# A two-layer transformer kernel whose softmax exponentials are shared by two engines: the first MLP weight streamed, two polynomial chains in flight, eight heads begun early, and a longer planned latency for a broadcast

## The chip, the cores and the metric

The kernel runs on one core of one Trainium2 chip. The metric is the device time of one launch in microseconds (us), median of several runs. The core has a matrix engine (TensorE, "PE" in the profile, "PEld" for its weight loads), a vector engine (VectorE, "DVE"), an activation engine (ScalarE, "ACT"), a general one (GpSimd, "POOL") and DMA queues; here almost all DMAs are issued from the sync queue ("SPq"). "PEclk" or "the granted clock" is the share of full clock that TensorE was given. The program gives each engine one order of instructions, and that order is fixed when it is built. In the traces a VectorE instruction that waits holds up those behind it (2.91 us at 465 us, shown in the prediction).

## The reference

Two identical layers; S = 2048 rows, D = 512, 32 heads of 16, MLP width 1792, bf16:

```python
def _A_ref(x, wqkv, wo):                     # attention
    qkv = (x @ wqkv).reshape(B, S, 3, H, Dh).transpose(2, 0, 3, 1, 4)
    q, k, v = qkv[0], qkv[1], qkv[2]
    scores = einsum("bhqd,bhkd->bhqk", q, k) * (Dh ** -0.5)
    o = einsum("bhqk,bhkd->bhqd", softmax(scores), v)
    return o.transpose(0, 2, 1, 3).reshape(B, S, D) @ wo
def _B_ref(x, w1, w2):                       # MLP
    return einsum("bsf,fd->bsd", maximum(einsum("bsd,df->bsf", x, w1), 0), w2)
for _ in range(2):
    x = x + _A_ref(layernorm(x), wqkv, wo)
    x = x + _B_ref(layernorm(x), w1, w2)
```

32 heads x 2048 x 2048 scores x 2 layers are 268 million exponentials: 4096 blocks of 128 x 512.

## The kernel before

The rows are cut into four chunks of 512. A *segment* is four heads of one chunk of queries over all 16 row blocks of keys: 64 score blocks. Three blocks make one ScalarE instruction. The kernel's source is a list scheduler: while it emits instructions it keeps a planned clock for PE and one for DVE (`now_pe`, `now_dve`), notes when each product will be ready, and picks the next instruction for each engine. The plan lives at build time alone; on the chip only the order is left of it. `mark` puts a product on the plan's clock, `at` asks for it:

```python
def mark(key, engine="dve", lag=0.0):
    made[key] = (engine, (now_pe if engine == "pe" else now_dve)[0] + lag)

def run_dve(until, musts):                   # which instruction VectorE gets next
    while True:
        can = [(0, m[1], m) for m in musts[:1]]
        if now_dve[0] < until:
            can += [(1, e[1], None) for e in list(evac)[:1]]
            for t in dve_q:
                ready = at(t["deps"], "dve")
                if ready is not None:
                    can.append((2, ready, t))
        ...                                  # [cut] those ready within 40 ns, by kind
```

The end of a segment: the sums of the softmax lie in four rows of the copied output `u`. They are gathered to 128 lanes (`c`), inverted, written back and broadcast to all lanes (`r`), then multiplied. The broadcast is planned to be there 5.5 us after the reciprocal:

```python
def copy():
    ...                                      # [cut] u <- ps_o
    nc.sync.dma_start(out=c[:], in_=sums)    # sums = u[lane:P:32, :]
    mark(("c", n), lag=2600.0)
def recip():
    nc.vector.reciprocal(out=c[:], in_=c[:])
    nc.sync.dma_start(out=sums, in_=c[:])
    nc.sync.dma_start(out=r[:], in_=bass.AP(tensor=sums.tensor, offset=sums.offset,
                      ap=[list(sums.ap[0]), [0, 32], [1, QS]]))
    mark(("r", n), lag=5500.0)
...
task(250, recip, [("r", n)], [("c", n)])
task(700, lambda: mul(0, QS), ots + [("m", n)], [("r", n)] + war)
```

VectorE takes some blocks off ScalarE, in pairs. `first_step` reads the scores; then a *chain* of five instructions on 128 x 1024 makes the exponential as a polynomial. Only one pair can be under way, and only in the first part of a segment:

```python
elif (not pairs and r <= LAST_PAIR
      and now_dve[0] + sum(...) < now_pe[0] + BACKLOG):   # [cut]
    half = 0
...
steps = ((690, bits dm), (1260, step dy), (1260, step dy), (1260, step de), (690, bits di))
task(cost, fn, [k], [...], place=n)          # chains go to the front of the queue
```

Layer 2 cannot start until the last chunk of layer 1 has passed its MLP and its keys and values are made. To fill that time, the first six "heads" (`NACC = 6` tiles of four heads each) of layer 2 run on the 12 row blocks of chunks 0 to 2 (*early* row blocks), their partial outputs are put into the chain's own buffers, and the four *late* row blocks follow in short segments of 16 blocks.

The softmax here doesn't subtract the row's maximum and nothing guards it: scores larger than these inputs give would overflow.

## Time and profile before

| | before |
|---|---|
| time, median of 4 runs in the rounds of the comparison | 1899.84 us (1899.27 to 1901.33) |
| profiled span, granted clock | 1896.0 us, 0.976 |
| exponentials on ScalarE: busy, idle before them | 1740.3 us, 20.9 us |
| VectorE busy, blocks taken from ScalarE | 1149.9 us (61%), 232 of 4096 |
| span = start + exponential loop + tail | 67.7 + 1761.2 + 67.0 |

The prediction below shows the lines. In a group line, "1740.3, 1589 | 20.9 <-PE" is busy us, mean ns of one, and us for which the engine stood idle just before, with what ended most of that idling.

### The profile page before, as it was taken

To read this page: it belongs to the slowest core of one execution; us is meant where nothing else is said; L and a number is where in the kernel's file an instruction comes from. 1 tells how busy PE (TensorE), PEld (TensorE's weight loads), DVE (VectorE), ACT (ScalarE), POOL (GpSimd) and SP (SyncE) were. 2 spreads that over 40 slices of the span, in tenths; PEclk is the share of its full clock that TensorE was granted. 3 is DMA by queue.
4 is the path that set the end of the run, shared out by engine and by line. 5 is a ranking of instruction groups with operands and counts; after the bars stand their busy time and mean duration, and the time that the engine had idled before them with its cause. 6 is when DMAs were issued, how large, how long until landed. Compare 5 with 4: busy or idle time off the path is not lost.

```text
span 1896.0 us, 29515 instructions
## 1 busy us (share of the span) xinstructions
PE 1654.1 (87%) x12867; PEld 520.5 (27%) x12867; DVE 1149.9 (61%) x1741; ACT 1764.1 (93%) x1407; POOL 2.4 (0%) x35
## 2 busy tenths in 40 slices
PE   4788888998989998999999878989988998899976
PEld 2222222222222222222222222222222222222222
DVE  4465657766676776776532335676657665666552
ACT  2799999999999999999999989999999999999950
POOL 0000000000000000000000000000000000000000
PEclk9899999999999999999999989999999999999998
DMA  4000000000000000000000010000000000000000
GB/s 166 1 12 7 13 13 13 8 12 12 11 9 13 13 10 10 13 13 13 10 3 1 4 30 11 13 12 10 19 15 13 7 15 21 13 8 12 21 10 11
DMA packets 34133, 29.39 MB, mean 16 GB/s; under 512 B 17492, under 2 KB 25428, under 8 KB 34004
## 3 DMA queue, kind: packets, MB, share of 16 engines
q1 hardware_dynamic: 32420, 25.94, 5.8%
q8 instruction: 100, 1.64, 0.4%
q10 hardware_dynamic: 1584, 1.57, 0.2%
q14 instruction: 29, 0.24, 0.0%
HBM read 7.86 MB, written 2.10 MB: 5 GB/s over the span
## 4 chain that ended last, share of the span: by engine, by line
ACT 83%; PE 8%; DVE 4%; DMA 3%; issue 1%; SPq 0%; DVEq 0%
ACT e L870 83%; PE ps_s L849 2%; DMA r<-u 2%; PE ps_f L347 2%; PE ps_s L347 2%; PE ps_o L668 1%; PE ps_s L789 1%; DMA u<-c 1%; DVE stats L364 1%; ACT xnT L783 0%; PE ps_s L401 0%; DVE ot L628 0%; DMA x<-in_A_x_dram 0%; DVE q L481 0%; DVE ktp L446 0%
## 5 line engine op out<-in xcount | busy, mean ns | idle before, releaser
L870 ACT ACTIVATE e<-ps_s 128x1536 bf16<-128x1536 f32 (+1 forms) x1366 | 1740.3, 1589 | 20.9 <-PE ps_s L849 19.8
L849 PE MATMUL ps_s<-q,ktp 32*128 32x512 bf16 x6503 | 720.3, 385 | 171.5 <-ACT e L870 135.7
L668 PE MATMUL ps_o<-e,vaug 128*32 128x512 bf16 x3864 | 547.2, 394 | 9.2 <-DVE u L617 7.2
L849 PEld LDWEIGHTS <-ktp 32*128 32x128 bf16 x6503 | 233.1, 92 | 633.7 <-issue 539.2
L707 DVE TENSOR_SCALAR di<-ps_s 128x512 int32<-128x512 f32 x232 | 159.7, 688 | 319.8 <-PE ps_s L849 319.1
L668 PEld LDWEIGHTS <-vaug 128*32 128x32 bf16 x4560 | 162.4, 93 | 466.3 <-issue 440.6
L738 DVE SCALAR_TENSOR_TENSOR dy<-dm 128x1024 f32<-128x1024 f32 x116 | 142.1, 1225 | 3.7
L738 DVE SCALAR_TENSOR_TENSOR de<-dy,di 128x1024 bf16<-128x1024 f32 x116 | 141.8, 1223 | 2.9
L738 DVE SCALAR_TENSOR_TENSOR dy<-dy,dm 128x1024 f32<-128x1024 f32 x116 | 141.7, 1221 | 2.6
L347 PE MATMUL ps_f<-w,ht 128*128 128x512 bf16 x406 | 120.0, 384 | 0.6 <-DVE x L528 0.5
L347 PE MATMUL ps_f<-xn2T,w 128*128 128x512 bf16 x400 | 117.7, 386 | 0.7
L514 DVE TENSOR_SCALAR ht<-ps_f 128x512 bf16<-128x512 f32 x99 | 68.2, 689 | 82.5 <-PE ps_f L347 81.0
L732 DVE TENSOR_SCALAR dm<-di 128x1024 int32<-128x1024 int32 x116 | 80.3, 692 | 3.5
L732 DVE TENSOR_SCALAR di<-di 128x1024 int32<-128x1024 int32 x116 | 80.3, 692 | 3.2
L668 PE MATMUL ps_o<-de,vaug 128*32 128x512 bf16 x464 | 79.3, 382 | 0.0
L347 PE MATMUL ps_f<-xnT,wqkv 128*128 128x512 bf16 x248 | 74.1, 390 | 1.2
L628 DVE SCALAR_TENSOR_TENSOR ot<-u,mask,r 128x512 bf16<-128x512 f32 (+1 forms) x67 | 48.4, 722 | 36.1 <-DMA r<-u 33.4
L347 PE MATMUL ps_f<-wo,ot 128*128 128x512 bf16 x224 | 67.7, 388 | 1.1
L617 DVE COPY u<-ps_o 128x512 f32<-128x512 f32 x58 | 40.0, 690 | 41.3 <-PE ps_o L668 41.2
L481 DVE TENSOR_SCALAR q<-ps_f,qmask 128x512 bf16<-128x512 f32 x68 | 48.6, 742 | 14.6 <-PE ps_f L347 14.5
L668 PE MATMUL ps_o<-di,vaug 128*32 128x512 bf16 x232 | 54.7, 391 | 0.0
L499 DVE TENSOR_TENSOR x<-x,ps_f 128x512 bf16<-128x512 bf16 x28 | 19.1, 684 | 57.6 <-PE ps_f L347 57.5
(67 smaller groups left out, 483.6 us busy)
## 6 DMA issues: line engine op xcount, KB each, us to landing
r<-u SPq DMA_DIRECT2D x63, 256.0 KB
w<-in_B_w_dram SPq DMA_DIRECT2D x2, 1792.0 KB
x<-in_A_x_dram SPq DMA_DIRECT2D x16, 128.0 KB
out_dram<-x SPq DMA_DIRECT2D x16, 128.0 KB
wqkv<-in_A_wqkv_dram ACTq DMA_DIRECT2D x3, 512.0 KB
c<-u SPq DMA_DIRECT2D x63, 8.0 KB
u<-c SPq DMA_DIRECT2D x63, 8.0 KB
wo<-in_A_wo_dram SPq DMA_DIRECT2D x1, 512.0 KB
```

The source lines that it names most:

```text
L347: nc.tensor.matmul(b, lhsT, rhs, start=(i == 0), stop=(i == n - 1))
L481: nc.vector.tensor_scalar(out=qbuf[n % 2][e][:], in0=b, scalar1=qmask[e][:, 0:1], scalar2=None, op0=ALU.mult,)
L499: nc.vector.tensor_add(out=x_t[tt][:], in0=x_t[tt][:], in1=b)
L514: nc.vector.tensor_scalar(out=ht[ft][:], in0=b, scalar1=0.0, scalar2=None, op0=ALU.max)
L617: nc.vector.tensor_copy(out=u[:], in_=ps_o[:])
L628: nc.vector.scalar_tensor_tensor(out=ot[t][:, a : a + w], in0=u[:, a : a + w], scalar=mask[e][:, 0:1], in1=r[:, a : a + w], op0=ALU.mult, ...
L668: nc.tensor.matmul(ps_o[32 * g : 32 * g + 32, :], vaug[sg["l"]][kb][:, 4 * sg["T"] + g, 2 * e : 2 * e + 32], rhs, start=g not in sg["begun ...
L707: first = nc.vector.tensor_scalar(out=di[:, half, :].bitcast(I32), in0=src, scalar1=EXP_BIAS, scalar2=0.0, op0=ALU.add, op1=ALU.max,)
L732: nc.vector.tensor_scalar(out=out[:].bitcast(I32), in0=di[:].bitcast(I32), scalar1=keep, scalar2=put, op0=ALU.bitwise_and, op1=ALU.bitwise_or,
L738: nc.vector.scalar_tensor_tensor(out=out[:], in0=x[:], scalar=c, in1=y[:], op0=ALU.add, op1=ALU.mult)
L849: nc.tensor.matmul(b[:, w, :], kt[32 * g : 32 * g + 32, kc : kc + P], qbuf[sg["n"] % 2][sg["e"]][32 * g : 32 * g + 32, :], start=True, sto ...
L870: ex = nc.scalar.activation(out=eb[:, :m, :], in_=b[:, :m, :], func=ACTF.Exp, scale=1.0 / (LOG2E * UNIT),)
```

## The change

Four things: W1 (1.8 MB) is no longer resident but streamed in blocks of 128 columns through four buffers; two chains may be outstanding, with a new rule for starting a pair; eight heads instead of six begin on the early row blocks; and the planned latency of the broadcast goes from 5.5 to 8.5 us. The intent is to move more blocks from ScalarE, which bounds the kernel, to VectorE. The diff, cut:

```diff
-    NACC = 6
+    NACC = 8
+    NW1 = 4
-    LAST_PAIR = 12
-    BACKLOG = 3000.0
+    SPREAD = 1.3
+    LATE = 0.0
+    BACKLOG = 6000.0
-    w1 = sb([P, NDC, DFF], BF16, "w1")
+    w1buf = [sb([P, NDC, P], BF16, f"w1_{n}") for n in range(NW1)]
-    di = sb([P, 2, QS], FP32, "di")
+    dis = [sb([P, 2, QS], FP32, f"di{n}") for n in range(2)]
-    acc = [x[:, k, :] for x in (dm, dy, di) for k in range(2)]
+    acc = [x[:, k, :] for x in [dm, dy] + dis for k in range(2)]
+    def load_w1(n):
+        if n < 2 * NQS * NF:
+            ft = n % NF
+            nc.sync.dma_start(out=w1buf[n % NW1][:],
+                in_=B_w1[:, ft * P : (ft + 1) * P].rearrange("(c p) f -> p c f", p=P))
+            mark(("w1", n), "pe", 4000.0)
     # [cut] h_group uses w1buf[n % NW1], and reloads it after its last matmul
-            mark(("r", n), lag=5500.0)
+            mark(("r", n), lag=8500.0)
     # [cut] di is handed on with the pair
-            task(cost, fn, [k], [key + (n - 1,)] if n else [], place=n)
+            task(..., place=sum("chain" in t for t in dve_q))
+            maker[k]["chain"] = True
-            elif (not pairs and r <= LAST_PAIR and now_dve[0] + sum(...) < now_pe[0] + BACKLOG):
-                half = 0
+            elif len(pairs) < 2:
+                queued = sum(t["cost"] for t in dve_q if "chain" in t)
+                ends = max(now_dve[0], now_pe[0] + 2600.0) + SPREAD * (queued + 5200.0)
+                waiting = sum(t["cost"] for t in dve_q if at(t["deps"], "dve") is not None)
+                if (ends < now_pe[0] + (21 - r) * 1280.0 + LATE
+                    and now_dve[0] + waiting < now_pe[0] + BACKLOG):
+                    half = 0
```

More of the change, by code (lines that the diff above doesn't have):

```diff
@@ L137 @@
     nc.sync.dma_start(out=wo[:], in_=A_wo[:, :].rearrange("(c p) f -> p c f", p=P))
-    nc.sync.dma_start(out=w1[:], in_=B_w1[:, :].rearrange("(c p) f -> p c f", p=P))
     nc.sync.dma_start(out=w2[:], in_=B_w2[:, :].rearrange("(c p) f -> p c f", p=P))
@@ L332, in run_all, with mm_group @@
         assert not (urgent or work)
-    def mm_group(mms, fin, makes, deps, per=2, cost=690):
+    def mm_group(mms, fin, makes, deps, per=2, cost=690, after=None):
         hold = {}
@@ L349, in piece @@
                     put_evac(cost, lambda: fin(b))
+                    if after:
+                        after()
             pieces.append((min(per, n - a), piece))
@@ L507, in o_group @@
         )
+    def load_w1(n):
+        if n < 2 * NQS * NF:
+            ft = n % NF
+            nc.sync.dma_start(
+                out=w1buf[n % NW1][:],
+                in_=B_w1[:, ft * P : (ft + 1) * P].rearrange("(c p) f -> p c f", p=P),
+            )
+            mark(("w1", n), "pe", 4000.0)
     def h_group(l, j, ft, war):
+        n = ((l * NQS + j) * NF + ft) % NW1
         def fin(b):
@@ L519, in h_group @@
         return mm_group(
-            [(w1[:, c, ft * P : (ft + 1) * P], xn2T[:, c, :]) for c in range(NDC)], fin,
-            [("h", l, j, ft)], all4("xnT", ("ln2", l, j)) + war,
+            [(w1buf[n][:, c, :], xn2T[:, c, :]) for c in range(NDC)], fin,
+            [("h", l, j, ft)],
+            all4("xnT", ("ln2", l, j)) + war + [("w1", (l * NQS + j) * NF + ft)],
+            after=lambda: load_w1((l * NQS + j) * NF + ft + NW1),
         )
@@ L705, in dve_block @@
     def dve_block(half, sg, kb, g, src, ex, recent):
+        di = dis[(pair_no[0] + (half == 0)) % 2]
         def first_step():
@@ L720, in first_step, with chain @@
             if half == 1:
-                chain(pairs[-1]["key"])
+                chain(pairs[-1]["key"], di)
         if half == 0:
-            assert not pairs
             pair_no[0] += 1
-            pairs.append({"sg": sg, "key": ("e", pair_no[0]), "blocks": []})
+            pairs.append({"sg": sg, "key": ("e", pair_no[0]), "blocks": [], "di": di})
         pairs[-1]["blocks"].append((kb, g))
         musts.append((690, now_pe[0] + PE_TO_DVE, first_step))
-    def chain(key):
+    def chain(key, di):
         def bits(out, keep, put):
@@ L750, in chain @@
             k = key + (n,) if n + 1 < len(steps) else key
-            task(cost, fn, [k], [key + (n - 1,)] if n else [], place=n)
+            task(cost, fn, [k], [key + (n - 1,)] if n else [], place=sum("chain" in t for t in dve_q))
+            maker[k]["chain"] = True
     def emit_pair():
@@ L756, in emit_pair @@
         halves = list(enumerate(p["blocks"]))
-        tops = di[:].bitcast(BF16)
+        tops = p["di"][:].bitcast(BF16)
         for rhs in (de, de, None):
@@ L760, in emit_pair @@
                 pv(p["sg"], kb, g, tops[:, half, 1::2] if rhs is None else rhs[:, half, :])
+    for n in range(NW1):
+        load_w1(n)
     for j in range(NQS):
@@ L859 @@
                 half = 1 if r == pair_at + 2 else None
-            elif (
-                not pairs
-                and r <= LAST_PAIR
-                and now_dve[0] + sum(t["cost"] for t in dve_q if at(t["deps"], "dve") is not None)
-                < now_pe[0] + BACKLOG
-            ):
-                half = 0
+            elif len(pairs) < 2:
+                queued = sum(t["cost"] for t in dve_q if "chain" in t)
+                ends = max(now_dve[0], now_pe[0] + 2600.0) + SPREAD * (queued + 5200.0)
+                waiting = sum(t["cost"] for t in dve_q if at(t["deps"], "dve") is not None)
+                if (
+                    ends < now_pe[0] + (21 - r) * 1280.0 + LATE
+                    and now_dve[0] + waiting < now_pe[0] + BACKLOG
+                ):
+                    half = 0
         if half is not None:
```

## The prediction

> **What bounds the kernel now.** I read the page from the top. First the busy shares, then the chain that ended last:
>
> ```profile
> PE 1654.1 (87%) x12867; PEld 520.5 (27%) x12867; DVE 1149.9 (61%) x1741; ACT 1764.1 (93%) x1407; POOL 2.4 (0%) x35
> ...
> ACT 83%; PE 8%; DVE 4%; DMA 3%; issue 1%; SPq 0%; DVEq 0%
> ...
> L870 ACT ACTIVATE e<-ps_s 128x1536 bf16<-128x1536 f32 (+1 forms) x1366 | 1740.3, 1589 | 20.9 <-PE ps_s L849 19.8
> ```
>
> ScalarE (ACT) does the exponentials, three score blocks of 128x512 per instruction, and is the bound: 1740.3 us of them with only 20.9 us of idle before them. The first starts at 67.7 us and the last ends at 1828.95, so the span of 1896.0 is 67.7 of start, 1761.2 of exponential loop (1740.3 + 20.9) and 67.0 of tail. PE's 87% is no rival in the loop: part of its score matmuls are repeats[...] (6503 run, 4096 needed), and its waits are for ACT (135.7 us). VectorE (DVE) already takes 232 of the 4096 blocks, in pairs.
>
> Next the price of a block on ACT. Groups of instructions by form, and the timeline of ACT in a stretch where every instruction has three blocks:
>
> ```profile
> L870 ACT ACTIVATE e<-ps_s 128x1536 bf16<-128x1536 f32 x1133 | 1597.6, 1662 | 16.2 <-PE ps_s L849 15.1
> L870 ACT ACTIVATE e<-ps_s 128x1024 bf16<-128x1024 f32 x232 | 286.2, 1234 | 4.7 <-PE ps_s L849 4.7
> ...
> 966.29 98.20 ACT L870 ACTIVATE e<-ps_s 128x1536 bf16<-128x1536 f32 x73
> ```
>
> The means (1662, 1234) overlap their neighbours, so they overstate the rate. The stretch gives 98.20/73 = 1.345 us for three blocks. From the total, (1740.3 - 1133 x 1.345 - 0.9)/232 = 0.93 us for two. A block moved off ACT is worth 0.416 us (0.428 by the difference of the means).
>
> Last, the 20.9 us of idle. Busy time in stretches of 10 us (fields: PE, PEld, DVE, ACT, POOL, clock, DMA) and the waits:
>
> ```profile
> 460.00:470.00 10.00, 7.09 (x67) 2.43 (x67) 6.74 (x12) 8.20 (x8) 0.00 (x0) 0.91 0.12 25
> 470.00:480.00 10.00, 10.00 (x59) 2.18 (x53) 4.05 (x7) 7.43 (x6) 0.00 (x0) 0.57 0.00 0
> ...
> 1070.00:1080.00 10.00, 8.55 (x57) 2.51 (x56) 4.63 (x7) 7.75 (x6) 0.00 (x0) 1.00 0.00 0
> ...
> 1120.00:1130.00 10.00, 6.65 (x48) 1.49 (x45) 7.33 (x11) 6.78 (x6) 0.00 (x0) 0.83 0.16 32
> ...
> DVE ot L628 <- DMA r<-u: 33.4, 6, 8.6
> ...
> 465.08 0.75 DVE L628 SCALAR_TENSOR_TENSOR ot<-u,mask,r 128x512 bf16<-128x512 f32 x1 [2.91 <-DMA r<-u]
> ...
> 466.49 0.39 PE L849 MATMUL ps_s<-q,ktp 32*128 32x512 bf16 x3 [2.72 <-DVE di L707]
> ```
>
> At 465 a DVE multiply waits for the broadcast of a softmax denominator (r<-u), the first exp step queues behind it, PE waits 2.72 us for that step, ACT starves, and PE's clock then falls to 0.57. The same cause is at 1260 (2.43 us of ACT idle) and in the late row blocks at 1100-1130 (1.07 + 1.16 + 3.22 = 5.45). The event at 460-500 costs 4.8. Together 12.7 us come from r. Another 2.25 us at 1070 is ACT waiting where layer 2 needs keys and values of the last chunk. The remaining 6 are clock dips and scraps (2.7 at 940-960).
>
> [...]the trace has 1221 to 1225 for the three polynomial steps. [...]The broadcast r has 4 outermost; the DMA row shows about 0.2 of 16 engines through it[...]. [...]matmuls go from 0.39 to 0.61 us after the stall.
>
> **The change, part by part.** The instruction order of both programs can be compared without running them.
>
> (1) More blocks on DVE: 133 pairs instead of 116, so 266 blocks, and 3830 on ACT in the same 1366 instructions (1099 of three, 266 of two, one of one). ACT: 1099 x 1.345 + 266 x 0.93 + 0.9 = 1726.4, so 13.9 us less, all on the path. DVE pays 17 x (4 x 0.69 + 3 x 1.223 = 6.43) = 109 us, to 1259 us, about 67%. By attention segment (64 blocks), most now have four or six DVE blocks instead of four. With six, ACT needs 15.33 x 1.345 + 6 x 0.93 = 26.2 us, and DVE work in the fullest, summed with durations of the trace, is 25 to 26. So DVE is locally full.
>
> (2) The scheduler now assumes 8.5 us instead of 5.5 between reciprocal and broadcast. In the trace the reciprocal ends at 456.49 and the multiply starts at 465.08: 8.59. So the plan now agrees with the chip. In the late row blocks the order changes as one would want: before, each reciprocal came after the previous segment's multiply (a serial loop of about 9.5 us against 7.2 us of exponentials per short segment); now it comes before it. I expect most of the 12.7 us back.
>
> (3) Eight heads instead of six begin on early row blocks: the early stretch grows from 6 x 16 x 1.345 = 129 us to 172, so the last MLP and the keys and values of the last chunk fit; the 2.25 us at 1070 should go. Its price, no DVE help in two more segments, is already in the 266.
>
> (4) W1 in blocks: 112 loads of 128 KB instead of one load. A block is refilled when its four matmuls have run and is needed three groups later. In the tail a group takes 22.8/14 = 1.63 us, so there are 4.9 us for it. x loads of the same size landed in 2.3 us at the start of the trace. Hidden: 0 us. The start: the W1 load was behind everything needed early in its queue: 0 us.
>
> (5) The tail, a cost I see only in the order. Chains have priority, so a reciprocal now stands behind the chains of the next segment: by summed durations 15 to 22 us after its segment's copy, where it was 7 to 9. At the very end the reciprocal of the last but one segment comes after the third chain of the last segment. Before, the last chain's dm step began 14.5 us before the last exponential's end. Now the last pair's second half is three slots (4.0 us) later, and 2.7 us of another chain stand in front: start at -7.7, 5.2 of chain, 0.75 of multiply, 0.25 of reciprocal: about -1.5. Plus 8.6 is +7.1, and the multiply of that segment stands before the final normalisation, which can start at about +7.9; before it started at 1830.15, which is +1.2. Cost 6.7 us, on the path.
>
> In mid-run the same lateness makes multiplies follow reciprocals with only 0 to 6 us of DVE work between, in some 40 of 63 cases. There DVE will visibly wait for r, 100 to 250 us in all. But it falls in the end of a segment, where no pair runs, and the plan knows it: I count it mostly as harmless.
>
> Idle in the loop: 20.9 - 12.7 - 2.25 = 6, and 4 by choice for a DVE that is locally full: 10. Sum: -13.9 (ACT work) - 10.9 (idle) + 6.7 (tail) = -18.1. 1899.5 - 18 = 1881.
>
> **Rivals.** *DVE becomes the bound.* For: 25 of 26.2 us in the fullest segments; a wait for r in front of a first exp step cost 2.7 us at 465. Against: at 74% load in chunks 1 and 2, ACT stood idle for almost nothing but the r event; the scheduler starts a pair only where 1.3 times its chain fits. If 30 segments lost 0.7 us each, 21 us: about 1898, no gain. *The tail is not delayed* (the last chain runs earlier than I reckon, or the wait overlaps): 1874; with no idle at all in the loop as well, 1864. That is the floor and still above 0.98 x 1899.5 = 1861.5. *W1 blocks land late,* behind a 6.6 us broadcast[...]: for, one queue carries both; against, three groups of slack and no broadcast in the last groups. A miss of 2 us per four groups in the tail would add 5: 1886.
>
> **Range and chances.** The ACT term is firm to 1 us. Idle may be 4 to 20, the tail 2 to 9. That gives 1870 to 1893. Faster by over 2% needs less than the floor: 0.02. Slower by over 2% would need 38 us of new stalls: 0.01.
>
> **What would show it.** Step 1: 1099 and 266 instructions, busy time of exponentials near 1726. Step 2: idle before them about 10 instead of 20.9, the stretch of late row blocks near 1.345 us per instruction, while DVE's wait for r grows well above 33.4. Step 3: no gap where layer 2 takes up the last chunk. Step 4: no PE wait on a W1 transfer. Step 5: about 8 us from the end of the last exponential to the shuffle of the last segment, and a tail near 74 instead of 67. It is wrong if PE's waits on the first exp step (5.5 us as a wait before the matmul) grow to tens of us, or if ACT's idle stays at 20.

## More of the kernel before

One thing must be kept in mind with this kernel: its time goes with PE's mean granted clock from run to run. The 12 runs of the kernel before in the last set of rounds range from 1895.94 us at a clock of 0.977 to 1905.06 at 0.970. So a few us are only read from medians of several runs.

## The result, and the profile after

The changed kernel takes 1879.59 us (median of 4 runs, 1876.83 to 1881.23) against 1899.84. The ratio is 0.9891, 95% interval 0.9874 to 0.9908. Ratios here are the mean time of one kernel's runs over the mean of the other's in the same rounds, so not quite the ratio of the medians quoted. The profiled run has a span of 1876.4 us at a clock of 0.979.

From the page of the changed kernel (busy times; the chain that ended last; two groups of instructions):

```profile
PE 1617.2 (86%) x12546; PEld 517.2 (28%) x12712; DVE 1244.0 (66%) x1864; ACT 1749.2 (93%) x1407; POOL 2.4 (0%) x35
...
ACT 84%; PE 10%; DVE 4%; DMA 2%; issue 1%; SPq 0%; DVEq 0%
...
L894 ACT ACTIVATE e<-ps_s 128x1536 bf16<-128x1536 f32 (+1 forms) x1366 | 1725.4, 1552 | 14.5 <-PE ps_s L871 13.4
...
L645 DVE SCALAR_TENSOR_TENSOR ot<-u,mask,r 128x512 bf16<-128x512 f32 (+1 forms) x67 | 48.1, 718 | 81.3 <-DMA r<-u 81.1
```

ScalarE is still the bound. Its work fell by 14.9 us (1740.3 to 1725.4), its idling by 6.4 (20.9 to 14.5). VectorE took 34 more blocks and its wait for the broadcast r rose from 33.4 to 81.1 us. The first exponential starts at 67.89 us and the last ends at 1807.80, which leaves a tail of 68.6. So the 19.6 us of span are -14.9 (work) - 6.4 (idle) + 1.6 (tail) + 0.2 (start), to rounding.

The same group by form, as in the prediction's second view:

```profile
L894 ACT ACTIVATE e<-ps_s 128x1536 bf16<-128x1536 f32 x1099 | 1535.1, 1637 | 12.4 <-PE ps_s L871 11.2
L894 ACT ACTIVATE e<-ps_s 128x1024 bf16<-128x1024 f32 x266 | 305.3, 1206 | 2.2 <-PE ps_s L871 2.2
```

1099 and 266 instructions, as the build order said. (The busy times of the forms overlap; only their joint 1725.4 is a length of time.)

The timeline of ScalarE, where a row joins instructions that follow each other without a gap (start, length, xcount, and the idle time before it):

```profile
445.39 431.37 ACT L894 ACTIVATE e<-ps_s 128x1536 bf16<-128x1536 f32 x343 [0.17 <-PE ps_s L871]
...
1154.51 1.45 ACT L894 ACTIVATE e<-ps_s 128x1536 bf16<-128x1536 f32 x1 [1.83 <-PE ps_s L871]
...
1167.78 640.02 ACT L894 ACTIVATE e<-ps_s 128x1536 bf16<-128x1536 f32 x513 [1.46 <-PE ps_s L871]
```

Both long rows run over the places of the old stalls at 465 and 1260 us: those are gone, and from 1167.78 to its last exponential ScalarE never stops. What idle is left lies mostly in three places: 5.75 us in the late row blocks (1132 to 1168), 4.6 at 901 to 916 and 2.0 at 936 to 940. At 901 PE waited 1.19 us for a copy on VectorE; after it the clock was 0.57 (mean of 900 to 910) and each instruction lost 0.49 us for a while. The 2.0 us at 936 come from a gather, as shown below.

The waits of the changed kernel (us in total, times, longest):

```profile
DVE ot L645 <- DMA r<-u: 81.1, 21, 8.6
DVE c L653 <- DMA c<-u: 37.5, 8, 7.4
ACT e L894 <- PE ps_s L871: 13.4, 21, 1.8
```

There is a new line: VectorE waited 37.5 us for the gather c (1.8 before). Seven of the eight waits (35.3 us) are in the late row blocks. There, by time:

```profile
1143.71 0.53 SPq L655 DMA_DIRECT2D r<-u  x1
1144.29 0.52 SPq L637 DMA_DIRECT2D c<-u  x1
...
1150.60 0.25 DVE L653 RECIPROCAL c<-c 128x16 f32<-128x16 f32 x1 [6.95 <-DMA c<-u]
1152.00 0.74 DVE L645 SCALAR_TENSOR_TENSOR ot<-u,mask,r 128x512 bf16<-128x512 f32 x1
1152.85 0.69 DVE L632 TENSOR_TENSOR u<-di,ps_o 128x512 f32<-128x512 f32 x1
1153.59 0.40 PE L685 MATMUL ps_o<-e,vaug 128*32 128x512 bf16 x4 [2.93 <-DVE u L632]
```

The 8 KB gather c is issued 0.6 us after a 256 KB broadcast r and reaches the reciprocal only 6.3 us later, about when that broadcast lands. (The gather issued at 1112.85, with no broadcast in flight, was there after 1.84 us.) VectorE stands 6.95 us in front of the reciprocal, so the copy of the next output (u) is late, PE waits 2.93 us for it, and ScalarE loses the 1.83 us seen above at 1154.51. The reciprocals of this stretch come at 1123.66, 1132.65, 1141.61, 1150.60, 1159.58 and 1168.56: every 9.0 us, where a short segment has 7.2 us of exponentials.

The eighth wait does the same at 935 us, outside the late row blocks. The gather was issued at 931.18, 2.8 us after a broadcast:

```profile
935.27 0.25 DVE L653 RECIPROCAL c<-c 128x16 f32<-128x16 f32 x1 [2.27 <-DMA c<-u]
...
935.86 0.58 PE L404 MATMUL ps_f<-ident,xn 128*128 128x128 bf16 x4 [1.40 <-DVE xnT L432]
```

A copy for PE stands behind the reciprocal, PE waits 1.40 us for it, and ScalarE loses 2.0 us in the next two gaps. So gathers behind broadcasts, with the slow clock that follows (0.70 from 1150 to 1160 us, 0.62 from 1160 to 1170, 0.75 from 936 to 942), account for 7.75 of the 14.5 us of idle.

The end of the loop. First before:

```profile
1813.75 15.20 ACT L870 ACTIVATE e<-ps_s 128x1024 bf16<-128x1024 f32 x12
...
1830.15 0.72 DVE L648 STREAM_SHUFFLE r<-u 128x512 f32<-128x512 f32 x1
...
1832.30 2.12 PE L347 MATMUL ps_s<-wo,ot 128*128 128x512 bf16 x9 [1.30 <-DVE ot L628]
...
1837.24 3.46 PE L347 MATMUL ps_s<-wo,ot 128*128 128x512 bf16 x8 [2.82 <-DVE x L499]
```

And after:

```profile
1784.48 23.32 ACT L894 ACTIVATE e<-ps_s 128x1024 bf16<-128x1024 f32 x19
...
1803.85 0.24 DVE L653 RECIPROCAL c<-c 128x16 f32<-128x16 f32 x1
...
1812.70 0.75 DVE L645 SCALAR_TENSOR_TENSOR ot<-u,mask,r 128x512 bf16<-128x512 f32 x1 [3.75 <-DMA r<-u]
1813.38 0.72 DVE L665 STREAM_SHUFFLE r<-u 128x512 f32<-128x512 f32 x1
...
1815.53 4.02 PE L348 MATMUL ps_s<-wo,ot 128*128 128x512 bf16 x9 [1.41 <-DVE ot L645]
...
1820.47 1.89 PE L348 MATMUL ps_s<-wo,ot 128*128 128x512 bf16 x8 [0.92 <-DVE x L502]
```

The shuffle, with which the last segment's normalisation starts, comes 1.2 us after the last exponential before, and 5.6 after: the reciprocal of the last but one segment is late and its broadcast stands in front. But the eight matmuls of an output group then take 1.89 us instead of 3.46: in the old tail PE ran them at about half the rate. PE wasn't faster in the tail as a whole (its mean clock there was 0.85 after and 0.84 before). The slow stretch fell on other matmuls: the nine before took 4.02 us instead of 2.12, and still the next group starts 7.1 us after the shuffle in both kernels.

### The profile page after: what moved, and what is told of

It reads as the page before. It is cut to its first block, busy times and chain, and to the rows that moved or that the text cites. A ratio compares the mean times of both kernels' runs of the same rounds, so it can differ in the third digit from the quotient of the medians.

```text
span 1876.4 us, 29319 instructions
## 1 busy us (share of the span) xinstructions
PE 1617.2 (86%) x12546; PEld 517.2 (28%) x12712; DVE 1244.0 (66%) x1864; ACT 1749.2 (93%) x1407; POOL 2.4 (0%) x35
## 4 chain that ended last, share of the span: by engine, by line
ACT 84%; PE 10%; DVE 4%; DMA 2%; issue 1%; SPq 0%; DVEq 0%
ACT e L894 83%; PE ps_s L871 3%; PE ps_o L685 2%; PE ps_f L348 2%; PE ps_s L348 2%; PE ps_s L811 1%; DMA c<-u 1%; DVE stats L367 0%; ACT xnT L805 0%; PE ps_s L404 0%; DMA r<-u 0%; DVE q L484 0%; DVE x L545 0%; DMA x<-in_A_x_dram 0%; DVE ht L529 0%
## 5 line engine op out<-in xcount | busy, mean ns | idle before, releaser
L894 ACT ACTIVATE e<-ps_s 128x1536 bf16<-128x1536 f32 (+1 forms) x1366 | 1725.4, 1552 | 14.5 <-PE ps_s L871 13.4
L871 PE MATMUL ps_s<-q,ktp 32*128 32x512 bf16 x6276 | 702.5, 384 | 170.2 <-ACT e L894 140.0
L726 DVE TENSOR_SCALAR di<-ps_s 128x512 int32<-128x512 f32 x266 | 182.9, 688 | 103.6 <-PE ps_s L871 101.2
L756 DVE SCALAR_TENSOR_TENSOR de<-dy,di 128x1024 bf16<-128x1024 f32 x133 | 162.6, 1223 | 7.2
L756 DVE SCALAR_TENSOR_TENSOR dy<-dm 128x1024 f32<-128x1024 f32 x133 | 162.5, 1222 | 2.9
L756 DVE SCALAR_TENSOR_TENSOR dy<-dy,dm 128x1024 f32<-128x1024 f32 x133 | 162.4, 1221 | 2.6
L645 DVE SCALAR_TENSOR_TENSOR ot<-u,mask,r 128x512 bf16<-128x512 f32 (+1 forms) x67 | 48.1, 718 | 81.3 <-DMA r<-u 81.1
L685 PE MATMUL ps_o<-de,vaug 128*32 128x512 bf16 x532 | 94.6, 382 | 0.0
L750 DVE TENSOR_SCALAR di<-di 128x1024 int32<-128x1024 int32 x133 | 91.8, 690 | 2.9
L750 DVE TENSOR_SCALAR dm<-di 128x1024 int32<-128x1024 int32 x133 | 91.5, 688 | 1.5
L348 PE MATMUL ps_f<-xnT,wqkv 128*128 128x512 bf16 x210 | 67.2, 388 | 6.1 <-issue 4.5
L685 PE MATMUL ps_o<-di,vaug 128*32 128x512 bf16 x266 | 66.2, 391 | 0.0
```

The costliest lines, as they stand in the source:

```text
L348: nc.tensor.matmul(b, lhsT, rhs, start=(i == 0), stop=(i == n - 1))
L645: nc.vector.scalar_tensor_tensor(out=ot[t][:, a : a + w], in0=u[:, a : a + w], scalar=mask[e][:, 0:1], in1=r[:, a : a + w], op0=ALU.mult, ...
L685: nc.tensor.matmul(ps_o[32 * g : 32 * g + 32, :], vaug[sg["l"]][kb][:, 4 * sg["T"] + g, 2 * e : 2 * e + 32], rhs, start=g not in sg["begun ...
L726: first = nc.vector.tensor_scalar(out=di[:, half, :].bitcast(I32), in0=src, scalar1=EXP_BIAS, scalar2=0.0, op0=ALU.add, op1=ALU.max,)
L750: nc.vector.tensor_scalar(out=out[:].bitcast(I32), in0=di[:].bitcast(I32), scalar1=keep, scalar2=put, op0=ALU.bitwise_and, op1=ALU.bitwise_or,
L756: nc.vector.scalar_tensor_tensor(out=out[:], in0=x[:], scalar=c, in1=y[:], op0=ALU.add, op1=ALU.mult)
```

## The experiments

My theory after the result was: two chains give ScalarE less to do, but they push each reciprocal back behind a chain, so that the multiply follows it closely. Whether that costs anything depends on the order of VectorE's instructions, and the order on the planned latency. With 8.5 planned and 8.6 measured, multiplies stand where a wait harms nobody. The rival was the prediction's own view: the latency is a small separate repair (12.7 us), and the chains and heads add their parts to it. The first eight runs undo or do one part each.

| label | what | blocks on VectorE | time, us | ratio to before [95%] | exp busy / idle |
|---|---|---|---|---|---|
| a1 | before + lag 8.5 | 232 | 1890.56 | 0.9948 [0.993, 0.9965] | 1739.6 / 15.2 |
| a2 | before + W1 streamed | 232 | 1906.87 | 1.003 [1.001, 1.005] | 1741.4 / 29.9 |
| a3 | before + eight heads | 224 | 1907.17 | 1.0035 [1.0019, 1.0052] | 1745.0 / 27.2 |
| a4 | before + two chains | 274 | 1967.44 | 1.0342 [1.0315, 1.0368] | 1734.0 / 94.6 |
| b1 | after, lag 5.5 | 260 | 1981.04 | 1.0424 [1.0397, 1.0451] | 1742.3 / 102.3 |
| b2 | after, one chain | 224 | 1903.68 | 1.0019 [0.9999, 1.0039] | 1744.6 / 21.6 |
| b5 | after, six heads | 276 | 1889.23 | 0.9941 [0.9922, 0.9959] | 1721.8 / 27.1 |
| b0 | after, W1 resident | 266 | 1884.42 | 0.9908 [0.989, 0.9925] | 1726.7 / 20.4 |
| b4 | after, r in four DMAs | 266 | 1957.71 | 1.029 [1.0262, 1.0319] | 1735.4 / 77.1 |
| d1 | after, last reciprocal first | 266 | 1880.07 | 0.9894 [0.9877, 0.9911] | 1725.4 / 14.5 |
| e1 | after, late gathers on GpSimd's queue | 266 | 1884.18 | 0.9914 [0.9899, 0.9929] | 1727.1 / 19.8 |
| f1 | after, lag 9.5 | 256 | 1880.31 | 0.9888 [0.9867, 0.9909] | 1728.0 / 6.8 |

All results were correct. The kernel before had medians of 1899.9 to 1900.5 in these rounds. Busy and idle are of the one profiled run.

**a1: the latency alone.**

```diff
-            mark(("r", n), lag=5500.0)
+            mark(("r", n), lag=8500.0)
```

> The kernel before with one number changed: the scheduler's assumed time from reciprocal to broadcast is 8.5 us instead of 5.5. Same 232 blocks on VectorE. Theory A (what the profile after suggests): the stalls at 460 and 1260 go (4.8 + 2.4 us of ScalarE idle), while the late row blocks keep their loss of about 5.5, because the gather c lands only when the previous broadcast r has landed, about 9 us per short segment whatever the order. So about 7 us faster, 1893, idle before the exponentials about 14. Theory B (my prediction): the late row blocks recover too, 12.7 us, 1887, idle about 8. Theory C (the lag is worth nothing, the gain is all blocks): 1900.

The time fell by 9.4 us by the medians, between the two numbers expected. VectorE waited for r once (8.6 us) instead of six times, and idle fell by 5.7. The late row blocks kept part of their loss: by the windows from 1100 to 1130 us, 3.06 us where it was 5.45. There VectorE now waits for the gather c instead (21.1 us in five places in the whole run), and the reciprocals come every 9.0 us instead of 9.5. And around the place where layer 2 takes up the last chunk, from 1060 to 1080 us, ScalarE idles 5.75 us where it idled 2.25. So the latency alone is worth about half of the gain in the kernel before.

**a2: W1 streamed alone** (the w1buf, load_w1 and h_group parts of the change).

> The kernel before with W1 streamed in blocks of 128 columns through four buffers, nothing else; 232 blocks on VectorE. Theory: the loads are hidden, within 2 us of the kernel before (1898 to 1902), and no wait of PE for a transfer. Rival: [...]waits of VectorE for r grow by 10 us or more and the time by 3 to 6 us.

PE's weight loads waited for a W1 block only twice, 0.5 us in all, and the wait for r was near the old one (37.6 us, 7 times). Yet the median is 7 us longer: the extra idle lies mostly at 1454 to 1470 and 1677 to 1690 us, where each instruction lost about 0.49 us as in the clock dip at 901 of the changed kernel (the mean clock from 1140 to 1840 us was 0.98, where the kernel before had 1.00 from 1140 to 1830), and at the old stall near 1264 (5.1 us, 2.4 before). One of six runs had 1899.11 us at a clock of 0.976, the others 1904.8 to 1909.6 at 0.968 to 0.972. That the clock dipped at just these places is my reading; what set it off I can't tell.

**a3: eight heads alone.**

```diff
-    NACC = 6
+    NACC = 8
+    dx = sb([P, 2, QS], FP32, "dx")
-    acc = [x[:, k, :] for x in (dm, dy, di) for k in range(2)]
+    acc = [x[:, k, :] for x in (dm, dy, di, dx) for k in range(2)]
```

> The kernel before with eight heads begun on early row blocks instead of six (a second pair of buffers only to hold the sums). 224 blocks on VectorE, so 8 x 0.416 = 3.3 us more of exponentials. Theory: the 2.2 us of idle where layer 2 takes up the last chunk go, but two more short late segments each run at about 9.0 instead of 7.2 us, 3.6 us: about 4 to 5 us slower, 1904. Rival (late segments not limited by the broadcasts, only the blocks count): 1901.

It costs, 3 us more than expected: eight blocks go back to ScalarE and the wait for r rises to 51.6 us.

**a4: two chains alone** (the second di buffer and the new rule; W1 resident, six heads, lag 5.5).

> The kernel before with two chains outstanding and the new rule for starting a pair; W1 whole, six heads, assumed lag still 5.5 us. 274 blocks on VectorE instead of 232: 42 x 0.416 = 17.5 us fewer of exponentials. Theory: reciprocals now come late, so the wrong lag stalls the engine in many more places than two: idle grows from 21 to 30 or more, and the tail by about 2; time about 1890 to 1896. Rival (the lag hardly matters with two chains): idle stays at 21, time about 1884.

The direction was right (it loses most of its own gain) but the size was far off: 67 us slower. VectorE waits 222.8 us for r in 49 places, and idle before the exponentials is 94.6 us.

**b1: the whole change with the old latency.**

```diff
-            mark(("r", n), lag=8500.0)
+            mark(("r", n), lag=5500.0)
```

> The changed kernel with the assumed lag set back from 8.5 to 5.5 us; 260 blocks on VectorE instead of 266 (2.5 us of exponentials). Theory after the run of chains alone: the lag is what makes two chains bearable, VectorE waits for r in some 50 places in front of first steps, idle before the exponentials is 80 us or more instead of 14.5, time 1940 to 1965. Rival (my sum of the prediction, where the lag was worth 7 to 13 us): about 1890 to 1895; then something else made chains alone slow.

Even more than expected: 101 us slower than the changed kernel. One of its longer events, in the timeline:

```profile
510.27 0.75 DVE L645 SCALAR_TENSOR_TENSOR ot<-u,mask,r 128x512 bf16<-128x512 f32 x1 [4.52 <-DMA r<-u]
510.94 0.68 DVE L449 CAST ktp<-ps_f 128x512 bf16<-128x512 f32 x1
511.68 1.86 PE L348 MATMUL ps_f<-xnT,wqkv 128*128 128x512 bf16 x4 [2.56 <-DVE ktp L449]
...
514.58 2.37 ACT L894 ACTIVATE e<-ps_s 128x1536 bf16<-128x1536 f32 x2 [3.55 <-PE ps_s L871]
```

The multiply waits 4.52 us for its broadcast. The evacuation of a finished matmul group (the copy ktp<-ps_f) stands behind it in VectorE's order, PE's next matmul into ps_f waits 2.56 us for that copy, and ScalarE then waits 3.55 for scores. The clock follows. Busy time in 10 us (PE, PEld, DVE, ACT, POOL, clock, DMA), first with the old latency:

```profile
510.00:520.00 10.00, 7.72 (x34) 1.60 (x34) 5.29 (x8) 5.70 (x5) 0.00 (x0) 0.54 0.00 0
```

and in the changed kernel:

```profile
510.00:520.00 10.00, 9.39 (x72) 2.80 (x73) 4.42 (x8) 10.00 (x9) 0.00 (x0) 1.00 0.09 19
```

VectorE is half idle in both. It isn't load that hurts but what stands behind the wait. In the whole run VectorE waited for r 244.3 us in 52 places, against 81.1 in 21, and the mean clock was 0.931 against 0.979.

**b2: the change with one chain at a time.**

```diff
-            elif len(pairs) < 2:
+            elif not pairs:
```

> The changed kernel with one pair outstanding instead of two (the new starting rule, lag, W1 stream and eight heads stay); 224 blocks on VectorE. Theory: 42 x 0.416 = 17.5 us more of exponentials, idle about the same or a few us less, so 1893 to 1898. Rival (the second chain gives back much of its blocks as stalls): 1885 to 1890.

Missed: 1903.68, slower than expected. Only 224 blocks are moved, and most instructions lose about 0.49 us each at 1449 to 1464 and 1671 to 1685 us, much as in a2. Beside the changed kernel the second chain is worth 24 us; by the two profiled runs ScalarE's work differs by 19.2 (1744.6 against 1725.4) and its idle by 7.1.

**b5: the change with six heads.**

```diff
-    NACC = 8
+    NACC = 6
```

> The changed kernel with six heads begun early instead of eight; 276 blocks on VectorE instead of 266, 4.2 us less of exponentials, and two late short segments fewer, each about 1.8 us over its exponentials. Theory: eight heads do not pay, this is 3 to 8 us faster than the changed kernel, 1872 to 1877. Rival (eight heads pay because layer 2 would wait for the last chunk): a gap of 2 us or more appears where layer 2 takes up the last chunk and the time is the same or higher, 1880 or more.

The rival was right here. There is one gap that the changed kernel doesn't have:

```profile
1069.14 1.45 ACT L894 ACTIVATE e<-ps_s 128x1536 bf16<-128x1536 f32 x1 [12.22 <-PE ps_s L871]
```

PE waits there for the keys of the last chunk. They come at the same time as in the kernel before (to 0.13 us), whose gap was 2.25 us. First that kernel, then this run:

```profile
1067.62 0.69 DVE L446 CAST ktp<-ps_f 128x512 bf16<-128x512 f32 x1 [1.56 <-PE ps_f L347]
```

```profile
1067.75 0.69 DVE L449 CAST ktp<-ps_f 128x512 bf16<-128x512 f32 x1 [1.96 <-PE ps_f L348]
```

But ScalarE, with fewer blocks to do, runs out of other work at 1056.92 instead of 1071.21. So with two chains six early heads no longer last until the keys are there.

**b0: the change with W1 resident** (both engines' orders identical to the changed kernel's).

> The changed kernel with W1 loaded once and kept, as before the change; the order of instructions on TensorE and VectorE is the same to the last one. Theory: 112 loads share [...]the issuing queue with the gathers and broadcasts and start waits and clock dips (the run of W1 streaming alone was 6 us slower): this is 3 to 8 us faster than the changed kernel, 1872 to 1877. Rival (the loads are hidden, and the 6 us of that run were chance dips of the clock): within 2 us of the changed kernel, 1878 to 1881.

No difference from streaming is shown: 1884.42, with runs from 1878.75 us (clock 0.977) to 1886.03 (0.973), and an interval that overlaps the changed kernel's. It also fits in memory, so streaming was not needed to make room for the second di.

**b4: the broadcast cut into four DMAs, each with 32 partitions outermost.**

```diff
-            nc.sync.dma_start(out=r[:], in_=<4 rows x 32 copies x 512>)
+            for k in range(4):
+                row = u[32*k+lane : 32*k+lane+1, :]
+                nc.sync.dma_start(out=r[32*k:32*k+32, :], in_=AP(row, [[partition], [0,32], [1,QS]]))
```

> The changed kernel with each broadcast r split into four transfers of 64 KB, one per group of 32 partitions[...]; every other instruction in the same order. Theory: [...]four issues of 0.53 us and a short transfer, reciprocal to multiply 5 to 6.5 us instead of 8.6; the late row blocks come off their 9 us rhythm to about 7.2, their idle of 5.8 us goes, VectorE's wait for r falls from 81 to below 50, and the end comes 2 to 3 us sooner: 6 to 9 us faster, 1871 to 1874. Rival[...]: r takes as long or longer, time 1880 or more.

The rival was right: r got slower, not faster.

```profile
1155.43 0.25 DVE L653 RECIPROCAL c<-c 128x16 f32<-128x16 f32 x1 [1.94 <-DMA c<-u]
...
1157.53 2.80 SPq L657 DMA_DIRECT2D r<-u  x4
...
1166.59 0.75 DVE L645 SCALAR_TENSOR_TENSOR ot<-u,mask,r 128x512 bf16<-128x512 f32 x1 [0.40 <-DMA r<-u]
```

From the end of the reciprocal (1155.68) to the multiply are 10.9 us, not 8.6. Issuing four takes 2.80 us instead of 0.5, and that accounts for the difference: from the end of the last issue (1160.33) to the multiply are 6.3 us, where the changed kernel has 6.2 (at its end, 1806.50 to 1812.70). And the packets of the queue (count, MB, share of 16 engines' time) took more, first in this run, for the same bytes:

```profile
q1 hardware_dynamic: 94808, 38.81, 21.1%
```

then in the changed kernel:

```profile
q1 hardware_dynamic: 91028, 38.79, 9.1%
```

More engines were busy (a share of 0.7 to 0.9 of the 16 from 1159 to 1162 us, where one broadcast of the changed kernel has 0.20 to 0.24), and the data were there no sooner after the last issue. One DMA with a longer outermost dimension was not tried, and why r came no sooner is not shown. The order of PE and VectorE is that of the changed kernel, and the plan says 8.5: so this is a second case of a chip slower than its plan (by 2.4 us), and it cost 78 us. It isn't a clean one, since the issuing queue and the DMA engines carry more: the wait for c rose too, from 37.5 to 49.9 us.

**d1: at the very end, the reciprocal of the last but one segment ahead of the chains.**

```diff
-                    can.append((2, ready, t))
+                    can.append((1.5 if "first" in t else 2, ready, t))
+            if sg is segs[-2]: maker[("r", n)]["first"] = True
```

> The changed kernel with one reciprocal moved: that of the last but one segment goes ahead of the chains of the last segment; nothing else on VectorE moves but one addition, and TensorE's order is the same. Theory: the last normalisation starts about 1.2 us after the last exponential instead of 5.6, and 3 to 5 us come off the tail, 1875 to 1877. Rival (the tail after it is set by TensorE's clock and takes back what is won): 1878 to 1880.

The edit did what it should. The last exponential ends at 1808.77 in this run, and:

```profile
1787.50 0.25 DVE L653 RECIPROCAL c<-c 128x16 f32<-128x16 f32 x1 [0.83 <-DMA c<-u]
...
1809.97 0.72 DVE L665 STREAM_SHUFFLE r<-u 128x512 f32<-128x512 f32 x1
```

The shuffle is at +1.2 us again instead of +5.6. But the layer norm after it starts 15.1 us after the last exponential, against 17.9, and the tail is 67.2 against 68.6: of 4.4 us 1.4 remain, as the rival expected, and the median doesn't show them.

**e1: the gathers of the late row blocks issued from GpSimd's queue.**

```diff
-                nc.sync.dma_start(out=c[:], in_=sums)
+                (nc.gpsimd if sg["load"] else nc.sync).dma_start(out=c[:], in_=sums)
```

> The changed kernel with the gather c of the eight late short segments (only these) issued from GpSimd's queue, which is idle, instead of SyncE's; order on TensorE and VectorE the same. Theory: the gather then need not stand behind the broadcast in flight[...], the rhythm of the reciprocals in the late row blocks falls from 9.0 us to 7.5 or less, and the 5.8 us of idle there go to 2 or less: 1874 to 1877. Rival (the gather waits[...] whatever its queue): rhythm 9 us, time 1879 or more.

The rival was right again:

```profile
1130.76 0.25 DVE L653 RECIPROCAL c<-c 128x16 f32<-128x16 f32 x1 [6.06 <-DMA c<-u]
1140.10 0.25 DVE L653 RECIPROCAL c<-c 128x16 f32<-128x16 f32 x1 [6.58 <-DMA c<-u]
1149.41 0.25 DVE L653 RECIPROCAL c<-c 128x16 f32<-128x16 f32 x1 [7.25 <-DMA c<-u]
```

9.3 us from one to the next instead of 9.0, and a wait for c of 39.1 us. In this run another queue didn't free the gather from a broadcast in flight. One gather of the eight shows what might: its issue began at 1160.59, 0.17 us before that of the broadcast and not after it, and it reached the reciprocal after 3.8 us, 5.7 us after the reciprocal before. No run makes this order on purpose.

**f1: a planned latency above the measured one.**

```diff
-            mark(("r", n), lag=8500.0)
+            mark(("r", n), lag=9500.0)
```

> The changed kernel with 9.5 us planned between reciprocal and broadcast in place of 8.5 (measured there: 8.6). It asks whether the gain needs the plan to hit the chip's latency, or only not to fall short of it. My theory (only a shortfall hurts, because an in-order VectorE then stands before a first exp step; a surplus only makes a multiply later than it could be): about 1880, within 1876 to 1886, VectorE's wait for the broadcast below the changed kernel's 81 us, perhaps 40 to 70, since multiplies are placed later, idle before the exponentials 12 to 20. A first rival (8.5 is itself a shortfall by 0.1 us and part of the remaining idle comes from it): 1872 to 1876 and idle below 10. A second rival (a surplus hurts too, as later multiplies hold back the two buffers of copies and so the segments): over 1890, idle over 25.

The theory's time holds: 1880.31, no different from 8.5. The wait for r did not fall as I expected but rose to 97.5 us (18 times, longest 8.6), with ten fewer blocks on VectorE. That wait is again harmless:

```profile
L894 ACT ACTIVATE e<-ps_s 128x1536 bf16<-128x1536 f32 (+1 forms) x1366 | 1728.0, 1570 | 6.8 <-PE ps_s L871 6.1
```

The idle of 6.8 is of a run with a clock of 0.984 (1873.35 us); four of the six runs had 0.974 to 0.976 and 1880 to 1883 us. No experiment beat the changed kernel.

## Why the prediction was right or wrong

The time (1881.0 predicted, 1879.59 measured) and the class were right. The sum was right partly by luck, because two wrong terms cancelled.

**Step 1, blocks: right.** 1726.4 predicted, 1725.4 measured; 34 blocks were worth 14.9 us, or 0.44 each. (VectorE's busy time came to 1244.0 us, not 1259.)

**Step 2, idle 10 us: too low; 14.5 measured.** What failed is "I expect most of the 12.7 us back" as far as it covers the late row blocks, and with it "the stretch of late row blocks near 1.345 us per instruction". The stalls at 460 and 1260 went, but the late row blocks lose 5.75 us where they lost 5.45. The order did change as I said: the reciprocal now comes before the previous multiply. I overlooked that it needs the gather c, and c lands with the broadcast in flight. The loop is still serial, at 9.0 us instead of 9.5 against 7.2. The same wait costs 2.0 us at 936. Another 4.6 us, a clock dip at 901 to 916, were not foreseen; about the sum of the two I had left for scraps.

The reason for the wait is not shown. Issued up to 2 us after a broadcast, c was seen 5.0 to 6.3 us after its issue, about when r landed (five gathers), against 1.84 us with none in flight; from another queue it took 5.8 to 7.0 us (four gathers in e1; the profile's median from issue to landing was 5.9 us on that queue from 1105 to 1160). No run shows which engines the gathers used.

The wait of VectorE for r "100 to 250 us" was too high (81.1, 21 times and not some 40), but "I count it mostly as harmless" holds, and f1 shows it once more with 97.5.

**Step 3, eight heads: right that the gap goes, wrong in what it is worth.** I set it at 2.25 us. With two chains ScalarE is at this place 14.3 us sooner, and the eight heads cover a gap of 12.22 (b5).

**Step 4, W1: right.** Hidden in the changed kernel, and resident is no faster (b0). That it cost 7 us alone in the kernel before (a2), with a mean clock of 0.968 to 0.972 in five of its six runs, stays unexplained.

**Step 5, the tail: the mechanism right, the size off.** "About +7.9" was +5.6, since the last reciprocal ended at -3.7 and not -1.5 (its chain started at -9.8, not -7.7); from there to the multiply are 8.6, as reckoned. The delay was 4.4 and not 6.7. And the tail "near 74" was 68.6: 2.8 of the 4.4 us came back, 1.6 of them in the group of eight matmuls that no longer fell into a slow stretch of PE. d1 confirms it from the other side: with the delay gone that group takes 3.54 us again. By the sum it should have been 73.7, so the tail came out 5.1 below its term, and the idle of step 2 came out 4.5 above its own: the two cancelled.

**One reading.** The "0.39 to 0.61 us" of the matmuls is read from rows of three score matmuls; the slow one (468.74) isn't among the lines that the prediction shows.

**What the steps missed together.** The prediction adds its parts. The runs show that they don't add:

| part | alone, in the kernel before | in the changed kernel, beside the same without it |
|---|---|---|
| latency 8.5 | -9 us (a1) | -101 us (b1) |
| two chains | +67 us (a4) | -24 us (b2) |
| eight heads | +7 us (a3) | -10 us (b5) |
| W1 streamed | +7 us (a2) | none shown (b0) |

(Differences of medians.) Two chains are a loss in a plan that thinks the broadcast is there at 5.5 us, and a gain in one that says 8.5. In b1 the order puts evacuations and first exp steps behind some 50 waits for r, and PE's mean clock falls on top (0.931 against 0.979). b4 makes a like loss with the order untouched and the chip slower. From 8.5 to 9.5 the time doesn't change (f1). So falling short of the chip was dear in these runs (by 2.4 us in b4, 3.1 in b1); going over by 1 us cost nothing that shows.

Open are what sets the 6.7 us from the issue of the broadcast to the multiply (four parts on more engines didn't shorten it), what sets off the clock dips outside the stalls (0.57 from 900 to 910 us in the changed kernel, where the kernel before had 1.00; and the mean clock changes from run to run, 0.970 to 0.977 in the kernel before), and how to break the loop of the late row blocks.

## What to carry to other kernels

Where a build-time plan orders an engine on which a wait holds up what stands behind it (as VectorE here, 2.91 us at 465 us), measure the latency of each asynchronous step in the trace and let the plan err to the long side (1 us of it was harmless here): a wait is priced by what stands behind it in the order, and not by its length. Test the parts of a change both alone and by taking each out of the whole, because a part that loses alone can be what the whole needs. And before counting on an overlap of two small transfers, check in the trace whether the second really lands before the first.
